# Outward part of a two-layer kernel: eight matmuls, not six, between the first pair of banks and the third pair's products

## The chip, the cores and the metric

One core of a Trainium2 chip runs the kernel. The metric is the device time in microseconds (us) of one execution, as the median of several runs. Differences below 0.2% (about 2.1 us here) can't be told from no change.

## The reference

Three stages run one after the other, all in float32:

```
scores = q @ k^T / sqrt(64) - log(448);  attn = sigmoid(scores);  x = attn @ v      # 4 batches, 12 heads, 448 x 64
x = reshape(x)                                # 1792 tokens x 768 channels
g = relu(x @ w_in)**2;             x = g @ w_out      # layer 0, hidden width 2048
h = x @ w2_in; g = max(h,0) + alpha*min(h,0); out = g @ w2_out   # layer 1, hidden width 2048
```

The document calls the product with w_in of a layer *inward* and the product with w_out *outward*.

## The kernel before, in words

The attention stage takes the first 158 us. The two layers are cut into 32 **units** (`UNITS`, numbered here 0 to 31): layer (2) x half of the tokens, 896 columns (2) x pair of 128-wide blocks of the hidden width (8). Units 0 to 15 are layer 0, units 16 to 31 are layer 1. Each unit has an inward part of 63 matmuls (`product`, L511: seven products k = 0 to 6 of nine matmuls, which give the four quarters of the hidden block pair by additions) and an outward part (`out_product`, L534) of 72 matmuls in layer 0 and 84 in layer 1.

Every operand is held as a high and a low part of type fp32r, so that one float32 product is three matmuls: high by high and high by low of the weights (`HIGH`, two matmuls), and low by high (`LOW`, one matmul). Hidden values are in `G[j]` (j = 0, 1 for the two hidden blocks; halves t = 0, 1 of the tokens), outward weights in `WO[j]`.

The outward results go in **pairs** of output tiles: six pairs per unit in layer 0, seven in layer 1. A pair fills two banks of PSUM, which are one buffer of `two`; there are two such buffers, used in turn. When a pair is complete, one instruction evicts both banks into the accumulator `acc`: L720 on VectorE (DVE) adds to it, L718 on ScalarE (ACT) copies where the unit is the first of its eight (units 0, 8, 16 and 24). So pair 2 (the third) takes the buffer of pair 0, and its first matmul has to wait for pair 0's eviction; pair 3 waits for pair 1's, and so on.

A complete pair needs 12 matmuls: two tiles x two hidden blocks x three. Of the first two pairs, the parts with j = 1 are issued ahead of those with j = 0. From the third pair on, each pair's 12 matmuls follow each other.

A hidden quarter is made on DVE and ACT once its product is out of TensorE (`add_hidden`): in layer 0 an addition (L662, DVE), relu, two squares (L642 to L644, ACT) and the low part `g` (L654, DVE); in layer 1 an addition (L662, DVE), two relus (L650, L651, ACT), a combination with alpha (L652, DVE), a copy to the high part (L653, ACT) and the low part (L654, DVE). The last quarter (from product k = 6: j = 1, t = 0) is made while the outward part has already begun; only pair 3 and later ones read the half t = 0. Weight parts for the next unit are made on the same engines: ACT L236 writes a high part, DVE L240 a low part, DVE L220 to L226 the sums (names `s12`, `s34`, `a1`, `a2`).

The order of instructions on each engine is written out by a planner (`class Plan`) when the program is built. TensorE (PE) keeps the order in which its jobs are added. On the other engines the planner simulates the program with assumed durations (0.2005 us per outward matmul in layer 0 and 0.1735 in layer 1; `dve(cols)` = 0.07 + 0.00105 cols; 0.17 us from the end of a PE job plus 0.10 before a reader may begin) and takes, of the jobs that are ready, the one with the earliest due time. It leaves an engine idle rather than begin a job that would still run when a job with an earlier due time becomes ready:

```
for j in now:
    end = t + jobs[j][1]
    if not any(due[s] < due[j] and begin(s, free[e]) < end and end > due[s] for s in soon):
        return t, j
```

A job counts as `soon` once the last of the jobs that it needs has begun. The due time of an eviction follows from the first matmul that reuses its buffer; that of a weight part from the next unit's products; that of the last quarter's jobs from pair 3. The chip then runs each engine's instructions strictly in the planned order, each when its semaphores allow.

Of the kernel before, what the change touches and what calls it, by code (L numbers as in the profile page):

```python
# [19 lines left out]
class Plan:  # L20
# [11 lines left out]
    def add(self, engine, us, emit, reads=(), writes=(), port=False, size=0):  # L32
        reads, writes = set(reads), set(writes)
        before = {self.last[k] for k in reads | writes if k in self.last}
        for k in writes:
            before |= self.readers.pop(k, set())
        me = len(self.jobs)
        before.discard(me)
        self.jobs.append((engine, us, emit, before, port, size))
        for k in writes:  # L40
            self.last[k] = me
        for k in reads:
            self.readers.setdefault(k, set()).add(me)
# [75 lines left out]
def fused_kernel(ctx: ExitStack, tc: tile.TileContext, q, k, v, w1i, w1o, w2i, w2o, alpha, out):  # L119
# [149 lines left out]
    with tc.manual_schedule():  # L269
# [6 lines left out]
        with tc.tile_pool(name="apool", bufs=1) as apool, tc.tile_pool(name="apsum", bufs=1, space=bass.MemoryType.PSUM) as psum:  # L276
# [145 lines left out]
            for what in X_ORDER[:-1]:  # L422
                i = int(what[1])
# [6 lines left out]
            for d in range(ND):  # L430
                u, w = 2 * d, 2 * d + 1
                i = d - 4
# [69 lines left out]
        HIGH, LOW = ((0, 0), (0, 1)), ((1, 0),)  # L502
# [10 lines left out]
        def outputs(n):  # L513

            if UNITS[n][0] == 0:
                return [[(c, t), (c + 1, t)] for t in (1, 0) for c in range(0, NC, 2)]
            return [[(m, 0), (m, 1)] for m in reversed(range(NM))]

        def sides(n, o):

            if UNITS[n][0] == 0:
                return [o[1]]
            return [t for t in range(2) if o[0] * P < (t + 1) * S and (o[0] + 1) * P > t * S]

        def out_product(n, o, ps, j, ways, begin, end):

            for i, (gi, wi) in enumerate(ways):
                if UNITS[n][0] == 0:
                    c, t = o
                    ops = WO[j][:, wi, c * P:(c + 1) * P], G[j][:, gi, t * S:(t + 1) * S]  # L530
                else:
                    m, e = o
                    ops = G[j][:, gi, m * P:(m + 1) * P], WO[j][:, wi, e * HALF:(e + 1) * HALF]
                nc.tensor.matmul(ps, *ops, start=(begin and i == 0), stop=(end and i == len(ways) - 1), skip_group_check=True)  # L534

        def part_of(n, os):
            layer, p, fp = UNITS[n]
            if layer == 0:
                c, t = os[0]
                cells = [((c + i) * 2 + t) * S // CELL + k for i in range(2) for k in range(S // CELL)]  # L540
                return values_of(p)[:, c:c + 2, t], cells
            m = os[0][0]
            return acc[p][:, m * DM:(m + 1) * DM].rearrange("p (e c) -> p e c", e=2), [m * DM // CELL + k for k in range(DM // CELL)]

        def store(col, rows, channels=slice(0, DM), queues=(nc.sync,)):

            i = at_queue = 0
            while i < P:
                b, at = divmod(col + i, S)
                to = out[b * S:(b + 1) * S, channels]  # L550
                if at < MAIN:
                    r, p = divmod(at, P)
                    n = min(P - i, P - p)
                    to = to[:MAIN].rearrange("(p r) c -> p r c", r=R)[p:p + n, r, :]
                else:
                    n = min(P - i, S - at)
                    to = to[at:at + n, :]
                queues[at_queue % len(queues)].dma_start(out=to, in_=rows[i:i + n])
                at_queue += 1
                i += n  # L560
# [4 lines left out]
        def act(cols):  # L565
            return 0.10 + 0.00083 * cols

        def dve(cols):
            return 0.07 + 0.00105 * cols
# [118 lines left out]
        def add_outward(n):  # L688

            layer, p, fp = UNITS[n]  # L690
            size = HALF if layer else S
            pairs = []
            for os in outputs(n):
                pairs.append((os, at_pair[0] % 2))
                at_pair[0] += 1

            def keys(o, j, ways):
                return [("g", j, t, gi) for gi, _ in ways for t in sides(n, o)] + [key for _, wi in ways for key in ([("wo", j, 0)] if wi == 0 else [("wo", j, 1, e) for e in range(2)])]

            def products(os, b, i, j, ways, begin, end):  # L700
                add("PE", len(ways) * PE_OUT[layer], lambda: out_product(n, os[i], two[b][:, i, :size], j, ways, begin, end), keys(os[i], j, ways), [("o", b)])

            for ways in (HIGH, LOW):
                for os, b in pairs[:2]:
                    for i in range(2):
                        products(os, b, i, 1, ways, ways is HIGH, False)
            for at, (os, b) in enumerate(pairs):
                for i in range(2):
                    if at < 2:
                        products(os, b, i, 0, HIGH + LOW, False, True)  # L710
                    else:
                        products(os, b, i, 0, HIGH + LOW, True, False)
                        products(os, b, i, 1, HIGH + LOW, False, True)
                part, cells = part_of(n, os)
                cells = [("acc", p, cell) for cell in cells]
                both = two[b][:, :, :size]
                if fp == 0:
                    add("ACT", act(2 * size), lambda part=part, both=both: nc.scalar.activation(part, both, AF.Copy), [("o", b)], cells)  # L718
                else:
                    add("DVE", dve(2 * size), lambda part=part, both=both: nc.vector.tensor_add(part, both, part), [("o", b), *cells], cells)  # L720
                if fp == NB - 1 and layer == 1:
                    m = os[0][0]
                    if n < NU - 1:
                        add("SP", 0.1, lambda m=m: store(p * PAIR + m * P, acc[p][:, m * DM:(m + 1) * DM]), cells, [], size=DM * BYTES)
                    else:
                        for e in range(2):
                            add("SP", 0.1, lambda m=m, e=e: store(p * PAIR + m * P, acc[p][:, m * DM + e * HALF:m * DM + (e + 1) * HALF], slice(e * HALF, (e + 1) * HALF), (nc.sync, nc.scalar)), cells, [], size=HALF * BYTES)
# [9 lines left out]
        for n in range(NU):  # L737
# [31 lines left out]
            if n < NU - NB and fp == NB - 1:  # L769
                for i in range(7):  # L770
                    if i < 4:
                        add("SP", 0.05, lambda i=i, to=x_kept[n // NB]: nc.sync.dma_start(out=X[i].bitcast(F32), in_=to[i]), [("x_kept", i, c) for c in range(KH)], [key for c in range(KH) for key in x_keys(i, c)], size=2 * KH * S * BYTES)
                    else:
                        for c in range(KH):
                            add_x_parts(other, i, c, "POOL" if i == 6 else "DVE", (X[i][:, 0, c], X[i][:, 1, c]), x_keys(i, c))
            add_outward(n)
        plan.run()

# [29 lines left out]
```

## Time and profile before

| | us |
|---|---|
| median of 3 runs (lowest, highest) | 1070.81 (1070.32, 1071.83) |
| the profiled execution's own time | 1072.4 |
| its span, first to last instruction | 1070.2 |
| PE busy / DVE busy / ACT busy / POOL busy | 1050.4 / 737.3 / 608.5 / 252.1 |
| mean granted TensorE clock | 0.998 |

A row of a timeline gives the start (us from the span's start), the duration of a group of consecutive like instructions, engine, line, operation, operands, count, and in brackets the idle time of the engine before it with what ended it. Matmuls are pipelined: a single one is shown as some 365 ns (448 columns) or 334 ns (384 columns) long although the next one starts some 200 or 174 ns later. So the idle time in brackets is smaller than the delay of the matmul behind it, which is its start less the start that the even pace would have given.

### The profile page before, as it was taken

To read this page: it belongs to the slowest core of one execution; us is meant where nothing else is said; L and a number is where in the kernel's file an instruction comes from. 1 tells how busy PE (TensorE), PEld (TensorE's weight loads), DVE (VectorE), ACT (ScalarE), POOL (GpSimd) and SP (SyncE) were. 2 spreads that over 40 slices of the span, in tenths; PEclk is the share of its full clock that TensorE was granted. 3 is DMA by queue.
4 is the path that set the end of the run, shared out by engine and by line. 5 is a ranking of instruction groups with operands and counts; after the bars stand their busy time and mean duration, and the time that the engine had idled before them with its cause. 6 is when DMAs were issued, how large, how long until landed. Compare 5 with 4: busy or idle time off the path is not lost. (4 is left out here: it accounts for less than half of the span.)

```text
span 1070.2 us, 14822 instructions
## 1 busy us (share of the span) xinstructions
PE 1050.4 (98%) x5607; PEld 912.3 (85%) x5607; DVE 737.3 (69%) x990; ACT 608.5 (57%) x933; POOL 252.1 (24%) x229
## 2 busy tenths in 40 slices
PE   9999999999999999999999999999999999999998
PEld 5555558888898989888898899999999999999997
DVE  5555976677677775777777686787666756666765
ACT  4567778667666558666565666554443463333432
POOL 0001323253311142542110335431111211111110
PEclk9999999999999999999999999999999999999999
DMA  7577738556655775676655844543115611111103
GB/s 150 147 190 196 199 106 291 156 177 212 228 194 158 260 278 182 201 270 220 202 207 192 324 167 170 184 170 121 48 49 214 207 59 60 60 60 59 51 9 104
DMA packets 126007, 174.78 MB, mean 163 GB/s; under 512 B 55536, under 2 KB 98800, under 8 KB 124272
## 3 DMA queue, kind: packets, MB, share of 16 engines
q1 hardware_dynamic: 123440, 172.59, 49.8%
q10 hardware_dynamic: 2496, 1.25, 0.4%
q8 instruction: 44, 0.72, 0.3%
q14 instruction: 27, 0.22, 0.1%
HBM read 123.87 MB, written 49.94 MB: 162 GB/s over the span
## 5 line engine op out<-in xcount | busy, mean ns | idle before, releaser
L511 PE MATMUL h<-x,wi 128*128 128x448 f32 x2016 | 419.9, 367 | 0.5 <-DVE c L662 0.4
L511 PEld LDWEIGHTS h<-x,wi 128*128 128x128 f32 x2016 | 378.0, 188 | 36.8 <-DVE c L662 1.2
L534 PE MATMUL o<-g,wo 128*128 128x448 f32 x1152 | 244.1, 369 | 10.0 <-DVE acc L720 8.8
L534 PEld LDWEIGHTS o<-g,wo 128*128 128x128 f32 x1152 | 216.2, 189 | 35.3 <-DVE acc L720 14.1
L534 PE MATMUL o<-wo,g 128*128 128x384 f32 x1344 | 240.7, 336 | 2.7 <-DVE acc L720 2.1
L534 PEld LDWEIGHTS o<-wo,g 128*128 128x128 f32 x1344 | 233.0, 188 | 8.8 <-DVE acc L720 6.7
L625 POOL TENSOR_TENSOR wo<-words_o,wo 128x384 fp32r<-128x384 f32 x128 | 128.8, 1038 | 416.6 <-ACT wo L628 369.3
L720 DVE TENSOR_TENSOR acc<-o,acc 128x768 f32<-128x768 f32 (+1 forms) x182 | 182.9, 1015 | 55.1 <-PE o L534 54.2
L662 DVE TENSOR_TENSOR c<-h,c 128x448 f32<-128x448 f32 x160 | 99.6, 623 | 164.6 <-PE h L511 160.6
L628 ACT ACTIVATE wo<-words_o 128x768 fp32r<-128x768 f32 x64 | 50.8, 838 | 188.0 <-issue 128.5
L654 DVE TENSOR_TENSOR g<-c,g 128x448 fp32r<-128x448 f32 x128 | 82.8, 656 | 25.6 <-ACT c L644 22.8
L352 ACT ACTIVATE a<-sc,bias 128x896 f32<-128x896 f32 x72 | 69.2, 1004 | 35.6 <-PE av L370 22.6
L264 POOL TENSOR_TENSOR stage<-acc,stage 128x448 fp32r<-128x448 f32 x36 | 45.3, 1258 | 183.2 <-ACT stage L261 183.2
L236 ACT ACTIVATE wi<-sums 128x768 fp32r<-128x768 f32 x64 | 53.3, 837 | 48.1 <-PE h L511 30.5
L190 ACT ACTIVATE raw<-raw 128x768 f32<-128x768 f32 x64 | 57.8, 904 | 16.0 <-DMA raw<-in_moe_w_in_dram 11.5
L240 DVE TENSOR_TENSOR wi<-sums,wi 128x768 fp32r<-128x768 f32 x64 | 61.0, 956 | 5.9 <-ACT wi L236 5.6
L370 PE MATMUL av<-a,v 128*64 128x448 f32 x288 | 59.4, 548 | 0.0
L192 ACT ACTIVATE raw<-raw 128x768 int32<-128x768 uint32 x64 | 57.6, 900 | 0.0
L650 ACT ACTIVATE pos<-c 128x448 f32<-128x448 f32 x48 | 27.8, 578 | 51.1 <-DVE c L662 50.2
L257 POOL TENSOR_TENSOR acc<-acc 128x448 f32<-128x448 f32 x40 | 53.6, 1348 | 11.4 <-DMA acc<-late 9.5
L240 DVE TENSOR_TENSOR wi<-words_i,wi 128x768 fp32r<-128x768 f32 x64 | 50.1, 786 | 6.6 <-ACT wi L236 4.7
L652 DVE SCALAR_TENSOR_TENSOR c<-c,nal,pos 128x448 f32<-128x448 f32 x64 | 43.4, 678 | 8.2 <-ACT c L651 8.0
(75 smaller groups left out, 847.0 us busy)
## 6 DMA issues: line engine op xcount, KB each, us to landing
raw<-in_moe_w_in_dram SPq DMA_DIRECT2D x32, 768.0 KB, 5.7
raw<-in_moe_w_out_dram SPq DMA_DIRECT2D x32, 768.0 KB, 5.2
kept_x<-stage SPq DMA_DIRECT2D x36, 448.0 KB, 3.5
x<-kept_x SPq DMA_DIRECT2D x12, 1344.0 KB, 11.2
v<-in_v_dram SPq DMA_DIRECT2D x24, 192.0 KB, 2.9
nat<-in_q_dram SPq DMA_DIRECT2D x22, 192.0 KB, 3.4
nat<-in_k_dram SPq DMA_DIRECT2D x20, 192.0 KB, 3.3
late<-held SPq DMA_DIRECT2D x12, 224.0 KB, 2.2
```

The lines of the kernel that those rows point to most:

```text
L190: nc.scalar.activation(half.bitcast(F32), half.bitcast(F32), AF.Prelu, scale=2.0 ** -112, alpha=2.0 ** 32)
L192: nc.scalar.activation(half, half.bitcast(U32), AF.Copy, scale=2.0 ** -29 * (1 - 2.0 ** -12), bias=-0.5 + 7.5 * 2.0 ** -12)
L240: nc.vector.tensor_sub(lo, w, hi)
L257: eng.tensor_sub(to, x, y)
L352: nc.scalar.activation(sig[u, j], ps[:, :, :S], AF.Sigmoid, bias=bias[:, :1], scale=SCALE)
L370: nc.tensor.matmul(avs[u][h * D:(h + 1) * D, :S], vals[u][:, h, j, :], a[:, h, :], start=(u % 2 == 0 and j == 0), stop=(u % 2 == 1 and j = ...
L511: nc.tensor.matmul(ps, W[:, wp, at:at + P], X[k][:, xp, c], start=(k < 3 and c == 0 and i == 0), stop=(c == KH - 1 and i == 2), skip_group ...
L534: nc.tensor.matmul(ps, *ops, start=(begin and i == 0), stop=(end and i == len(ways) - 1), skip_group_check=True)
L625: nc.gpsimd.tensor_sub(WO[j][:, 1, at], words["o"][:, j, at], WO[j][:, 0, at])
L654: add("DVE", dve(S), lambda: nc.vector.tensor_sub(gl, e, gh), [key, h_key], [l_key], port=True)
L662: add("DVE", dve(S), lambda: nc.vector.tensor_add(to, bank(b), other), [("h", b), other_key], [key])
L720: add("DVE", dve(2 * size), lambda part=part, both=both: nc.vector.tensor_add(part, both, part), [("o", b), *cells], cells)
```

## The change

The order of the first 24 outward matmuls of every unit is changed, and nothing else. Before: HIGH parts with j = 1 of pairs 0 and 1 (8 matmuls), their LOW parts (4), pair 0's six matmuls with j = 0, pair 1's six. After: HIGH parts with j = 1 of pairs 0 and 1 (8), then pair 0's LOW parts (2) and its six with j = 0, then pair 1's LOW parts (2) and its six. So pair 0 is complete after 16 matmuls, not 18, and pair 1 after 24 as before. All other engines' jobs are the same, and the planner orders them anew.

```diff
-            for ways in (HIGH, LOW):
-                for os, b in pairs[:2]:
+            for os, b in pairs[:2]:
+                for i in range(2):
+                    products(os, b, i, 1, HIGH, True, False)
+            for at, (os, b) in enumerate(pairs):
+                if at < 2:
                     for i in range(2):
-                        products(os, b, i, 1, ways, ways is HIGH, False)
-            for at, (os, b) in enumerate(pairs):
+                        products(os, b, i, 1, LOW, False, False)
                 for i in range(2):
                     if at < 2:
                         products(os, b, i, 0, HIGH + LOW, False, True)
```

## Rows read from the trace of the kernel before

**Rows 1.** Waits of PE: line, releaser, us in total, times, longest.
```profile
PE o L534 <- DVE acc L720: 11.0, 25, 2.4
```
**Rows 2.** Chain that ended last, around unit 26: start, us, engine, tile, line.
```profile
913.72 0.56 DVE wi L240
914.27 0.88 DVE acc L720
```
**Rows 3.** Timeline of PE, units 9 and 26, the next inward part last.
```profile
430.20 5.02 PE L534 MATMUL o<-g,wo 128*128 128x448 f32 x24
435.74 10.00 PE L534 MATMUL o<-g,wo 128*128 128x448 f32 x48 [0.52 <-DVE acc L720]
445.58 12.93 PE L511 MATMUL h<-x,wi 128*128 128x448 f32 x63
...
910.69 4.33 PE L534 MATMUL o<-wo,g 128*128 128x384 f32 x24
915.20 10.69 PE L534 MATMUL o<-wo,g 128*128 128x384 f32 x60 [0.18 <-DVE acc L720]
925.73 13.18 PE L511 MATMUL h<-x,wi 128*128 128x448 f32 x63
```
**Rows 4.** Timeline of DVE, units 9 and 26.
```profile
434.06 0.62 DVE L654 TENSOR_TENSOR g<-c,g 128x448 fp32r<-128x448 f32 x1 [0.59 <-ACT c L644]
434.60 2.08 DVE L720 TENSOR_TENSOR acc<-o,acc 128x896 f32<-128x896 f32 x2
...
912.96 0.68 DVE L652 SCALAR_TENSOR_TENSOR c<-c,nal,pos 128x448 f32<-128x448 f32 x1
913.72 0.56 DVE L240 TENSOR_TENSOR wi<-words_i,wi 128x384 fp32r<-128x384 f32 x1
914.19 1.82 DVE L720 TENSOR_TENSOR acc<-o,acc 128x768 f32<-128x768 f32 x2
915.93 1.15 DVE L654 TENSOR_TENSOR g<-c,g 128x448 fp32r<-128x448 f32 x2
```
**Rows 5.** Timeline of DVE, unit 31: its first two evictions.
```profile
1054.23 2.00 DVE L720 TENSOR_TENSOR acc<-o,acc 128x768 f32<-128x768 f32 x2 [0.49 <-PE o L534]
```
**Rows 6.** Timeline of DVE, unit 1, and of DVE, unit 14.
```profile
204.04 0.62 DVE L654 TENSOR_TENSOR g<-c,g 128x448 fp32r<-128x448 f32 x1 [0.73 <-ACT c L644]
...
576.20 0.56 DVE L240 TENSOR_TENSOR wi<-words_i,wi 128x384 fp32r<-128x384 f32 x1 [0.53 <-ACT wi L236]
```
**Rows 7.** Timeline of ACT, unit 0, ahead of and with its first eviction.
```profile
175.94 0.83 ACT L236 ACTIVATE wi<-sums 128x768 fp32r<-128x768 f32 x1
176.68 0.89 ACT L718 ACTIVATE acc<-o 128x896 f32<-128x896 f32 x1
```
**Rows 8.** Timeline of PE, units 2 and 3, and the inward part behind.
```profile
237.08 7.53 PE L534 MATMUL o<-g,wo 128*128 128x448 f32 x36 [0.53 <-DVE acc L720]
...
257.21 5.02 PE L534 MATMUL o<-g,wo 128*128 128x448 f32 x24
264.61 11.70 PE L534 MATMUL o<-g,wo 128*128 128x448 f32 x48 [2.38 <-DVE acc L720]
276.15 13.18 PE L511 MATMUL h<-x,wi 128*128 128x448 f32 x63
```
**Rows 9.** Timeline of DVE, unit 3.
```profile
261.24 0.96 DVE L240 TENSOR_TENSOR wi<-words_i,wi 128x768 fp32r<-128x768 f32 x1
262.93 0.62 DVE L654 TENSOR_TENSOR g<-c,g 128x448 fp32r<-128x448 f32 x1 [0.73 <-ACT c L644]
```
**Rows 10.** Windows, unit 3: stretch, length, busy (PE, PEld, DVE, ACT, POOL), clock, DMA.
```profile
264.61:267.30 2.69, 2.69 (x8) 2.41 (x9) 2.27 (x3) 2.69 (x5) 0.00 (x0) 0.58 0.03 6
```
**Rows 11.** Timelines of unit 17: DVE, POOL, PE.
```profile
662.90 2.80 DVE L654 TENSOR_TENSOR g<-c,g 128x448 fp32r<-128x448 f32 x2
...
663.80 2.91 POOL L257 TENSOR_TENSOR acc<-acc 128x448 f32<-128x448 f32 x2
...
665.76 7.75 PE L534 MATMUL o<-wo,g 128*128 128x384 f32 x43 [0.45 <-DVE g L654]
```

## The prediction

> **What bounds the kernel now.** I read the busy times first: PE is busy for 1050.4 of 1070.2 us, DVE for 737.3 and ACT for 608.5, so only what delays PE can move the end. Then the waits of PE: nearly all of them are outward matmuls that wait for an eviction on DVE, 25 waits and 11.0 us [rows 1]. The chain of waits says the same for one unit: a weight part on DVE, then the eviction, then 60 matmuls [rows 2].
>
> The waits understate it, since a matmul is drawn longer than the distance to the next. The timeline of PE gives the true delay. In unit 26 (layer 1) the first 24 matmuls last 4.33 us; less one matmul's 0.334 and divided by 23 that is a pace of 0.1737. The 25th should start at 910.69 + 24 x 0.1737 = 914.86 and starts at 915.20: 0.34 late. The 60 from there to the inward part take 925.73 - 915.20 = 10.53, 0.11 more than 60 x 0.1737. So the unit loses 0.45 [rows 3]. In unit 9 (layer 0) the pace is (5.02 - 0.365) / 23 = 0.2024, the 25th is 435.74 - 435.06 = 0.68 late, and the same 0.11 follows: 0.79 [rows 3]. This sum over the 32 units gives 20.3 us, of which unit 3 has 2.6.
>
> **Why the eviction is late: the order on DVE.** In unit 26 pair 0's last matmul is drawn until 913.98 (start 910.69, 17 paces, one matmul of 0.334), yet the first of the two evictions, each some 0.96 long, begins at 914.19, behind a weight part of 0.56 that began at 913.72 [rows 4]. In unit 9 pair 0 is through by 434.01, and the eviction begins at 434.60 behind the low part of the last quarter, which had come at 434.06 after 0.59 of idling [rows 4]. Only where DVE has nothing else, as in unit 31, does it begin at once: 1054.23, when pair 0 is through at 1054.20 [rows 5].
>
> **The change, step by step.**
>
> *Matmuls.* None is added or removed, each has its own weight load before and after: 0. Operands: the parts with j = 0 are wanted two matmuls (0.35 to 0.41) sooner, pair 1's LOW parts later. In unit 26 all that these read was made before the outward part began or in its first 0.4 us, against 10 matmuls = 1.74 us: 0. Only unit 0, whose last such low part comes closest, may lose up to 0.2.
>
> *Two matmuls more of cover.* Pair 0 is complete 2 x 0.1737 = 0.35 (layer 1) or 0.40 (layer 0) sooner. If the eviction then begins at once, it is over in unit 26 at 910.69 + 2.94 + 0.03 + 0.96 = 914.62, ahead of the 25th matmul's 914.86 and about when its weight load would go. In unit 9: 430.20 + 3.41 + 0.03 + 1.09 = 434.73, against 435.06. So stall and the 0.11 behind it (a weight load that isn't hidden) both vanish: not 0.35 but all of 0.45 or 0.79.
>
> *Does it begin at once?* That hangs on the planner, by its own assumed times (used for the order only). Layer 0: the eviction used to become ready 18 x 0.2005 + 0.27 = 3.88 after the first outward matmul, now 3.48. The low part of the last quarter takes 0.54 in its reckoning; in the planner's listing of the kernel before it begins between 2.98 and 3.32 in units 3 to 7 and 9 to 13, so it would end after 3.48. An eviction with an earlier due time then holds it back (the quoted loop), and DVE takes the eviction first. In units 1, 14 and 15 the low part begins at 2.61 to 2.81 and stays ahead. In units 14 and 15 another job (from 3.76) stood between it and the eviction; this one now goes behind. Layer 1: ready at 16 x 0.1735 + 0.27 = 3.05, not 3.39; the combination L652 of the last quarter (2.53 to 3.14 in the listing) and the weight part (3.27) both go behind it.
>
> *The sum for layer 0*, from each unit's delay as above: units 4 to 7 and 9 to 13 lose nothing any more, nine units of 0.36 to 0.79, together 5.8. Units 14 and 15 (weight part or x part ahead of the eviction [rows 6]) 2.2. Unit 1: the low part runs at 204.04, after pair 0 would be through, and the eviction stays behind it [rows 6]: 0. Units 0 and 8, where ACT evicts: the weight copy of 0.83 ahead [rows 7] goes behind; ACT is free only at about 175.9, so 0.75 and 0.5. Unit 2: DVE is free 0.46 sooner, and the second eviction, now behind a weight part (0.76 of delay before the 37th matmul [rows 8]), goes ahead of it: 1.2. Unit 3: the 25th matmul is 264.61 - 262.07 = 2.5 late, since the low part comes at 262.93 only [rows 8, 9]. With the eviction behind the weight part of 261.24, which lasts until 262.2, about 1.3 remains. The ten matmuls after the stall run at a granted clock of 0.58 [rows 10], near the lower of the two levels (1.2 of 2.4 GHz), and cost 1.6; nothing like it follows delays of up to 1 us elsewhere. I take that clock loss as gone: 2.8 (bounds 1.3 and 3.0). Layer 0: 13.2.
>
> *The sum for layer 1.* Eleven units with a job between (18, 20 to 23, 25 to 30), nine of 0.45, one 0.53, one 0.56: 5.1. Units 16, 24 and 31: 0.8. Units 17 and 19: 0, next paragraph. Layer 1: 5.9.
>
> *What is late next.* The last quarter's chain goes behind the eviction. In unit 26 L652 moves from 912.96 to about 914.5 and the two low parts end about 917.2, against 917.08 before [rows 4]. Pair 3's LOW part, the 42nd matmul, is due at 910.69 + 41 x 0.1737 = 917.81, its weight load at 917.6: 0.4 of slack. In unit 17 it is gone already: the two low parts take 2.80 instead of 1.15, while POOL works (663.80), and the 42nd matmul waits for them [rows 11]. There the gain is given back, in units 17 and 19. The Trainium skill (SBUF — State Buffer, Who interferes with whom) has a rule that makes more of this: a DVE instruction with two SBUF inputs contends with a GpSimd instruction that reads SBUF, one with at most one SBUF input does not. By it the evictions, which read PSUM, never stretch, while L652 and L654, which the change moves later, stretch wherever POOL is at work, units 17 to 19; with unit 18 given back too the sum would be 0.5 less.
>
> *Pace.* Matmuls of 448 columns run in one of two paces that last until a stall: (12.93 - 0.365) / 62 = 0.2027 in one inward part [rows 3], (13.18 - 0.368) / 62 = 0.2066 in another [rows 8]. Which comes after a stall I can't foretell. Without stalls from unit 4 on one pace would hold for 12 x 135 = 1620 matmuls, of which some 900 now have the faster: all slow costs 3.5, all fast gives 2.8. I take 0.
>
> *Total.* 13.2 + 5.9 = 19.1, less 1.6 for small new waits that another order brings (bounds 0 and 4): 17.5. The profiled execution took 1072.4, 1.6 above the median of 1070.8; 1072.4 - 17.5 = 1054.9 there, 1053.3 for the median. I say 1053.5.
>
> **The rivals.**
>
> 1. *The order on the engines stays.* The eviction is ready sooner but still stands behind the low part or the weight part. For it: 0.35 to 0.4 is little, and the parts that stand ahead begin 0.03 and 0.26 us before or around pair 0's end [rows 4]. Against it: the planner's rule, and its margins (3.48 falls inside the span of the low part in ten units; only unit 13's margin is as small as 0.04). Only units 16, 17, 19, 24 and 31 would gain, 1.4 in all: 1069.4. The Trainium skill (TensorE: Matmul & The Clock Gate, Architectural detail) says that ACT and DVE are strict first-in first-out: by that, the case hangs on the written order alone.
>
> 2. *Stalls move from the 25th to the 42nd matmul in layer 1.* If L652 goes behind both evictions (1 us later still), the low parts end about 918.0 and the 42nd matmul is 0.3 late: of 5.9 only 1 or 2 remain, and layer 0 with its pace slow gives 9.5: about 1060.
>
> 3. *Slower.* As in 2, but with ACT taking two weight copies (0.83 each) before the copy L653, since the quarter comes so late. The low part would end 1.7 us later, about 919.7, the 42nd matmul 2.0 late instead of the 0.45 now: 16 x 1.55 = 25 lost against 13 gained, 1083. It decides from the point at which the low part ends more than 1.7 us after 917.08, and the whole kernel is slower from 1.3 of new delay per unit. Against it: L653's due time is by far the earlier.
>
> 4. *Pace* all slow or all fast: 1057 or 1050.5, within the forecast's own range.
>
> **How the numbers follow.** Forecast (order flips in most units, 1048 to 1059): 0.72. Rival 1: 0.11. Rival 2: 0.09. Rival 3: 0.05. Below 1048 (all of the 20 and the fast pace): 0.03. The range for 8 in 10 takes in the forecast and most of rival 2: 1048 to 1064. Faster by over 0.2% (about what a measurement can tell from no change): forecast, rival 2, below, and a little of rival 1: 0.86. Same: 0.09. Slower: 0.05.
>
> **What would show it.** Right: in unit 26's place the first eviction starts 0.03 after the 16th matmul's end with the last quarter's L652 and the weight part behind it; PE's waits for L720 fall from 11.0 to under 3; unit 1 keeps its stall; unit 3's clock stays full. Wrong: evictions that still begin behind L654 or L240, or a new row of waits of PE for L654.

## The result, and the profile after

The changed kernel takes 1059.14 us as the median of 4 runs (1058.57 to 1059.38), the kernel before 1071.15 beside it: ratio 0.9887, 95% interval 0.987 to 0.9905, so 12.0 us less. The forecast was 1053.5 with a range of 1048 to 1064: right in direction and inside the range, but 5.6 us too hopeful. The profiled execution took 1058.57, its span 1056.8, 13.4 less than before.

The waits of PE in the changed kernel (the eviction on DVE is now line 722, that on ACT line 720):

```profile
PE o L534 <- DVE acc L722: 3.4, 6, 1.1
PE h L511 <- DVE c L662: 2.7, 4, 1.0
PE o L534 <- ACT acc L720: 1.8, 2, 1.3
```

Against [rows 1], the waits for DVE evictions fell from 11.0 to 3.4 (the prediction had named under 3 as the sign of being right). New is the second row: inward matmuls that wait for DVE additions, 0.4 us before.

Layer 1 went nearly as foreseen. Timelines of PE and of DVE in unit 26, to be held against [rows 3, 4]:

```profile
899.21 14.85 PE L534 MATMUL o<-wo,g 128*128 128x384 f32 x84
913.90 1.40 PE L511 MATMUL h<-x,wi 128*128 128x448 f32 x6
```
```profile
901.82 0.63 DVE L654 TENSOR_TENSOR g<-c,g 128x448 fp32r<-128x448 f32 x1 [0.26 <-ACT g L653]
902.36 0.95 DVE L722 TENSOR_TENSOR acc<-o,acc 128x768 f32<-128x768 f32 x1
903.23 0.68 DVE L652 SCALAR_TENSOR_TENSOR c<-c,nal,pos 128x448 f32<-128x448 f32 x1
903.82 0.95 DVE L722 TENSOR_TENSOR acc<-o,acc 128x768 f32<-128x768 f32 x1
```

The 84 matmuls need 913.90 - 899.21 = 14.69 us, 15.04 before; at the even pace it would be 14.59. The weight part is gone from in front of the eviction, and L652 has gone behind it. But another job stands there now: the low part of the quarter from k = 5 (L654), so the eviction starts at 902.36 and not at 902.18. It ends in time for the 25th matmul (903.38), not for its weight load, which idles 0.15 us and begins at 903.37, just after the eviction's end at 903.31; the 26th matmul is 0.10 late. This 0.10 is left in ten units, 0.18 to 0.24 in units 17 to 19, nothing in 16, 24 and 31.

Layer 0 split in two. In units 2, 3, 4, 6 and 10 the eviction went ahead of the last quarter's low part and the delay is gone, but for 0.16 in unit 3. Unit 10, PE and then DVE of unit 2:

```profile
454.10 14.76 PE L534 MATMUL o<-g,wo 128*128 128x448 f32 x72
468.69 1.58 PE L511 MATMUL h<-x,wi 128*128 128x448 f32 x7
```
```profile
232.51 1.09 DVE L722 TENSOR_TENSOR acc<-o,acc 128x896 f32<-128x896 f32 x1 [0.50 <-PE o L534]
233.52 0.61 DVE L654 TENSOR_TENSOR g<-c,g 128x448 fp32r<-128x448 f32 x1
234.12 1.09 DVE L722 TENSOR_TENSOR acc<-o,acc 128x896 f32<-128x896 f32 x1
```

468.69 - 454.10 is 72 times 0.2026: nothing lost, and in unit 2 DVE waited for PE, not PE for DVE. In units 5, 7, 9 and 12 to 15 (and in unit 1, as forecast) the last quarter's low part kept its place. In unit 11 it went behind, but a weight part for which DVE idled 1.15 us stands there instead, and the delay grew from 0.78 to 1.00. In units 0 and 8, where ACT evicts, 0.73 and 1.58 are left. Unit 12, PE, DVE and ACT:

```profile
509.81 15.11 PE L534 MATMUL o<-g,wo 128*128 128x448 f32 x72
524.76 5.44 PE L511 MATMUL h<-x,wi 128*128 128x448 f32 x26
```
```profile
511.56 0.96 DVE L240 TENSOR_TENSOR wi<-words_i,wi 128x768 fp32r<-128x768 f32 x1
513.25 0.62 DVE L654 TENSOR_TENSOR g<-c,g 128x448 fp32r<-128x448 f32 x1 [0.73 <-ACT c L644]
513.79 1.08 DVE L722 TENSOR_TENSOR acc<-o,acc 128x896 f32<-128x896 f32 x1
```
```profile
511.43 0.56 ACT L642 ACTIVATE c<-c 128x448 f32<-128x448 f32 x1
512.02 0.58 ACT L643 ACTIVATE g<-c 128x448 fp32r<-128x448 f32 x1
512.64 0.58 ACT L644 ACTIVATE c<-c 128x448 f32<-128x448 f32 x1
```

Pair 0 was through at 513.22. DVE idled 0.73 us for ACT, then made the low part, then evicted, 0.57 late. The unit takes 524.76 - 509.81 = 14.95, 0.36 more than unit 10.

To see where the time went I took the starts of all matmuls of the units and compared each distance with 0.2027 (448 columns) or 0.1735 (384): what the 25th and 26th matmul of an outward part are late; other gaps over 0.045 us; and the rest, which is the slower pace. In us, good to about 0.1, from the profiled execution of each:

| kernel | median | 25th, layer 0 | 25th, layer 1 | other gaps | slower pace |
|---|---|---|---|---|---|
| before | 1071.15 | 13.7 | 6.6 | 4.6 | 7.2 |
| changed | 1059.14 | 8.5 | 1.6 | 4.3 | 4.2 |
| x1_order | 1061.95 | 9.1 | 4.3 | 2.8 | 6.1 |
| x2_cover | 1070.19 | 13.7 | 5.8 | 5.0 | 6.4 |
| x3_act | 1047.47 | 0.3 | 0.3 | 3.7 | 3.4 |
| x4_twelve | 1050.76 | 0.3 | 0.0 | 5.8 | 4.6 |
| x5_act_six | 1059.05 | 4.9 | 4.7 | 3.6 | 6.5 |
| x6_nopool | 1049.98 | 2.0 | 1.8 | 1.0 | 4.1 |
| x8_act_twelve | 1052.36 | 0.0 | 0.0 | 6.4 | 4.8 |
| x9_act_nopool | 1051.85 | 0.0 | 0.6 | 2.2 | 5.2 |
| x10_memset | 1053.13 | 5.0 | 1.5 | 0.5 | 5.7 |

From before to changed: 5.2 + 5.0 + 0.3 + 3.0 = 13.5, the 13.4 of the span.

The medians were taken on several chips, on which the kernel before took 1070.11 to 1071.41. The ratios given below are each to the kernel before on the same chip, so two experiments are best compared by their ratios (0.001 is 1.1 us).

### The profile page after: what moved, and what is told of

Read it like the earlier page. It is cut to its first block, busy times and chain, and to the rows that moved or that the text cites. A ratio compares the mean times of both kernels' runs of the same rounds, so it can differ in the third digit from the quotient of the medians.

```text
span 1056.8 us, 14833 instructions
## 1 busy us (share of the span) xinstructions
PE 1041.5 (99%) x5607; PEld 911.7 (86%) x5607; DVE 744.0 (70%) x990; ACT 606.8 (57%) x933; POOL 254.0 (24%) x229
## 4 chain that ended last, share of the span: by engine, by line
PE 82%; ACT 9%; DVE 4%; DMA 2%; issue 2%; SPq 0%; POOL 0%; ACTq 0%; DVEq 0%
PE o L534 39%; PE h L511 30%; PE av L370 5%; PE sc L350 4%; ACT g L643 2%; ACT c L644 2%; ACT c L642 2%; ACT wi L236 1%; PE tp L317 1%; PE av L378 1%; DVE acc L722 1%; PE scr L360 1%; DVE c L662 1%; PE tp L320 1%; DMA raw<-in_moe_w_in_dram 1%
## 5 line engine op out<-in xcount | busy, mean ns | idle before, releaser
L511 PE MATMUL h<-x,wi 128*128 128x448 f32 x2016 | 419.1, 367 | 2.7 <-DVE c L662 2.7
L511 PEld LDWEIGHTS h<-x,wi 128*128 128x128 f32 x2016 | 378.0, 188 | 38.3 <-DVE c L662 4.8
L534 PE MATMUL o<-g,wo 128*128 128x448 f32 x1152 | 239.4, 367 | 5.4 <-DVE acc L722 3.4
L534 PE MATMUL o<-wo,g 128*128 128x384 f32 x1344 | 237.6, 336 | 0.0
L625 POOL TENSOR_TENSOR wo<-words_o,wo 128x384 fp32r<-128x384 f32 x128 | 130.2, 1049 | 394.4 <-ACT wo L628 391.4
L662 DVE TENSOR_TENSOR c<-h,c 128x448 f32<-128x448 f32 x160 | 99.4, 622 | 139.5 <-PE h L511 130.7
L654 DVE TENSOR_TENSOR g<-c,g 128x448 fp32r<-128x448 f32 x128 | 80.9, 632 | 33.7 <-ACT c L644 27.4
L264 POOL TENSOR_TENSOR stage<-acc,stage 128x448 fp32r<-128x448 f32 x36 | 46.4, 1288 | 188.4 <-ACT stage L261 164.2
L240 DVE TENSOR_TENSOR wi<-sums,wi 128x768 fp32r<-128x768 f32 x64 | 63.7, 997 | 8.0 <-ACT wi L236 7.6
L257 POOL TENSOR_TENSOR acc<-acc 128x448 f32<-128x448 f32 x40 | 54.8, 1372 | 10.8 <-DMA acc<-late 8.7
L240 DVE TENSOR_TENSOR wi<-words_i,wi 128x768 fp32r<-128x768 f32 x64 | 52.0, 814 | 6.4 <-ACT wi L236 4.8
L652 DVE SCALAR_TENSOR_TENSOR c<-c,nal,pos 128x448 f32<-128x448 f32 x64 | 43.4, 678 | 7.7 <-ACT c L651 7.5
```

What stands on the lines that cost most here:

```text
L240: nc.vector.tensor_sub(lo, w, hi)
L511: nc.tensor.matmul(ps, W[:, wp, at:at + P], X[k][:, xp, c], start=(k < 3 and c == 0 and i == 0), stop=(c == KH - 1 and i == 2), skip_group ...
L625: nc.gpsimd.tensor_sub(WO[j][:, 1, at], words["o"][:, j, at], WO[j][:, 0, at])
L654: add("DVE", dve(S), lambda: nc.vector.tensor_sub(gl, e, gh), [key, h_key], [l_key], port=True)
L662: add("DVE", dve(S), lambda: nc.vector.tensor_add(to, bank(b), other), [("h", b), other_key], [key])
```

## The experiments

**Order or cover?** Two kernels take the change apart. In x1_order the planner sees the changed order, but PE issues pair 1's LOW matmuls where they stood before; in x2_cover it is the other way round.

Against the changed kernel, in x1_order pair 1's LOW jobs issue nothing, and pair 0's first job with j = 0 issues them:

```diff
+                    if how == "first":
+                        for other in early.pop("low"):
+                            other()
+                    if how != "done":
                         out_product(n, os[i], two[b][:, i, :size], j, ways, begin, end)
```

Against the kernel before, in x2_cover pair 1's first job with j = 0 issues them:

```diff
+                    if how == "first":
+                        for c in range(2):
+                            out_product(n, os[c], two[b][:, c, :size], 1, LOW, False, False)
```

> DVE, ACT and POOL run in the order that the planner wrote for the changed kernel, PE in the order of the kernel before (pair 0 complete after 18 matmuls, six of cover). Theory (the new order on DVE carries most of the gain): every first eviction starts no sooner than pair 0's end, 0.35 to 0.40 us later than in the changed kernel where it started at once there; layer 0 keeps its delays and adds about 0.2 in five units, layer 1 has about 0.28 a unit instead of 0.10: some 4 us above the changed kernel, 1063, 8 below the kernel before. Rival (the two matmuls of cover carry it): about the kernel before, 1069 to 1071.

> PE in the order of the changed kernel (pair 0 complete after 16 matmuls), DVE, ACT and POOL in the order that the planner wrote for the kernel before. Theory (order): evictions stay behind the low part in layer 0 and the weight part in layer 1, so the 25th matmul is late as before; only units 16, 17, 19, 24 and 31 gain, 1.4 us together: about 1069.5. Rival (cover): 0.35 to 0.40 in each of 32 units, 11 to 12 us: about 1059.

x1_order: 1061.95, ratio 0.992 (0.9908 to 0.9932), 8 us below the kernel before. x2_cover: 1070.19, ratio 0.9997 (0.9988 to 1.0006), no gain. The order of the other engines alone brings two thirds of the change, the two matmuls alone nothing, and the remaining 4 us come only where both are there. DVE in unit 9 of x2_cover shows why (the eviction is line 727 here):

```profile
432.95 0.95 DVE L240 TENSOR_TENSOR wi<-sums,wi 128x768 fp32r<-128x768 f32 x1
434.50 0.63 DVE L654 TENSOR_TENSOR g<-c,g 128x448 fp32r<-128x448 f32 x1 [0.60 <-ACT c L644]
435.04 2.08 DVE L727 TENSOR_TENSOR acc<-o,acc 128x896 f32<-128x896 f32 x2
```

The sequence is that of [rows 4], idle time and all: a pair that is ready sooner changes nothing for an instruction that stands behind another. In units 17, 19 and 31, where nothing stood ahead, the delays of 0.28 to 0.35 did go to nothing; units 16 and 24, which the expectation also named, gained nothing.

**Why seven units of layer 0 kept the old order.** In the traces a relu and the two squares behind it start some 0.60 us apart on ACT (511.43, 512.02 and 512.64 in unit 12 above); the planner reckons 0.47.

```diff
-                ready[s] = max(ready[s], t + us if jobs[s][0] == e and e != "SP" else end + self.HOP)
+                ready[s] = max(ready[s], t + us + (0.13 if e == "ACT" else 0.0) if jobs[s][0] == e and e != "SP" else end + self.HOP)
```

> The changed kernel; only the planner is told that an ACT job which needs the ACT job before it begins 0.13 us later, as the traces show (relu to square to square start 0.60 apart where the planner assumes 0.47). Theory (ten units of layer 0 keep their delay since the planner believes the last quarter's low part is done before the eviction is ready, and on the chip it comes 0.9 us later): with the longer chain the low part ends after 3.48 in the planner's time, the eviction goes ahead of it in most of those units, and PE's waits for L722 fall from 3.4 to under 1.5: 4 to 6 us less than the changed kernel, about 1054. Rival (the delays there have another cause, such as weight parts or DMA): within 1 us of the changed kernel.

1047.47, ratio 0.979 (0.9774 to 0.9806): 11.7 below the changed kernel by the medians, 10.4 by the ratios, twice the expectation. Layer 0 alone gained 8.2 at the 25th matmul, units 0, 8 and 11 with it, layer 1 gained 1.3 and the pace 0.8. The 25th matmul is late in two units only, 0.6 us in all. Unit 12, DVE:

```profile
503.23 0.62 DVE L654 TENSOR_TENSOR g<-c,g 128x448 fp32r<-128x448 f32 x1
504.93 1.09 DVE L722 TENSOR_TENSOR acc<-o,acc 128x896 f32<-128x896 f32 x1 [1.09 <-PE o L534]
505.94 0.61 DVE L654 TENSOR_TENSOR g<-c,g 128x448 fp32r<-128x448 f32 x1
506.56 1.09 DVE L722 TENSOR_TENSOR acc<-o,acc 128x896 f32<-128x896 f32 x1
```

DVE now waits for pair 0, evicts, and only then makes the last low part. The same correction with six matmuls of cover:

> The kernel before with its order of matmuls (six of cover); only the planner is told of the 0.13 us between dependent ACT jobs. Theory (what decides is which side of the low part the planner puts the eviction): the low part then ends after 3.88 in the planner's time in most units of layer 0, evictions go ahead of it, and the 25th matmul is 0.2 to 0.3 late instead of 0.8; unit 3's clock loss goes too: stall sum 8 to 10 instead of 20.3, about 1057. Rival (the correction helps only where the cover is eight): the order stays, 1068 to 1071.

1059.05, ratio 0.9884 (0.9864 to 0.9905): as much as the change itself, without its order of matmuls. Most units lose 0.2 to 0.35, the eviction's own length beyond six matmuls (unit 2 loses 1.5). So with the planner corrected, the two more matmuls, with the order that the planner then writes for them, are worth 11.6 us by the medians and 10.1 by the ratios; with the order of before they were worth nothing.

**More cover.** Pairs 0 and 1 one after the other.

```diff
-            for os, b in pairs[:2]:
-                for i in range(2):
-                    products(os, b, i, 1, HIGH, True, False)
             for at, (os, b) in enumerate(pairs):
                 if at < 2:
+                    for i in range(2):
+                        products(os, b, i, 1, HIGH, True, False)
```

> Pairs 0 and 1 one after the other, so that pair 0 is complete after 12 matmuls and 12 stand between. Theory: the eviction is ready 0.8 us (layer 0) or 0.7 (layer 1) sooner than in the changed kernel, ahead of the last quarter's low part in every unit; the delay of the 25th matmul is gone nearly everywhere (10.1 us in the changed kernel), but pair 0 now wants the low part of j = 0, t = 1 at the 9th matmul, 1.6 us after the first, which in units 0 and 3 comes later than that: 7 to 9 us below the changed kernel, about 1051. Rival (new waits for hidden values at the 7th to 9th matmul, and evictions that push the hidden chain back): no gain or a loss, 1058 to 1064.

> Corrected planner and twelve matmuls of cover together. Theory (x3_act has already lost all but 0.6 us of the delay of the 25th matmul, so cover is worth nothing more): within 2 us of x3_act, 1046 to 1050. Rival (cover and order are separate gains that add): 1040 or less.

x4_twelve: 1050.76, ratio 0.9826 (0.9806 to 0.9847), as expected: with twelve the delay is gone though the planner is wrong. With both corrections, x8_act_twelve: 1052.36, ratio 0.9833 (0.9795 to 0.9871), no better than x3_act and 2.4 outside what was expected. Its delay at the 25th matmul is zero, but its other gaps are 6.4, of which 2.3 are waits for low parts (L654). Cover and order are two ways to the same gain.

**The new waits of inward matmuls.** In unit 10's inward part PE waits a microsecond for L662. PE, DVE and POOL there:

```profile
448.52 5.74 PE L511 MATMUL h<-x,wi 128*128 128x448 f32 x27 [1.01 <-DVE c L662]
```
```profile
444.51 1.52 DVE L222 TENSOR_TENSOR sums<-sums,words_i 128x384 f32<-128x384 f32 x1
445.95 1.51 DVE L224 TENSOR_TENSOR sums<-words_i 128x384 f32<-128x384 f32 x1
447.39 0.54 DVE L226 TENSOR_TENSOR sums<-words_i,sums 128x384 f32<-128x384 f32 x1
447.86 0.61 DVE L662 TENSOR_TENSOR c<-h,c 128x448 f32<-128x448 f32 x1
```
```profile
444.47 1.15 POOL L264 TENSOR_TENSOR stage<-acc,stage 128x448 fp32r<-128x448 f32 x1
445.69 1.36 POOL L257 TENSOR_TENSOR acc<-acc 128x448 f32<-128x448 f32 x1
```

Three like sums take 1.52, 1.51 and 0.54 us; the two long ones lie beside POOL instructions. That the rule of the Trainium skill which the prediction names (SBUF — State Buffer, Who interferes with whom) would strike here, in the inward part, I had not seen. The trace agrees with it: 1.5 us beside POOL instructions that read, 0.54 without. x10_memset keeps every order and lets POOL only write where it made the x sums and the kept x parts (the low parts of outward weights, L625, it still computes):

```diff
-            add(engine, ..., lambda: x_sum(p, i, c, nc.gpsimd if engine == "POOL" else nc.vector), ...)
+            add(engine, ..., lambda: nc.gpsimd.memset(x_block(p, X_SUM[i][0], c), 0.0), ...)
...
-            add(engine, ..., lambda: x_low(p, i, c, hi, lo, ...), ...)
+            add(engine, ..., lambda: nc.gpsimd.memset(lo.bitcast(F32), 0.0) if engine == "POOL" and i < 4 else x_low(p, i, c, hi, lo, ...), ...)
```

> The changed kernel with the same order of instructions on every engine; only the x sums (L257) and the low parts of x into stage (L264) on POOL are replaced by fills with zero, which read nothing. It leaves out that part of the second half's input. Theory (DVE sums with two operands in SBUF stretch from 0.55 to 1.5 us while a POOL instruction reads SBUF, and this is what delays L662 and makes inward matmuls wait in units 2, 3, 10 and 18): the sums L220 to L226 stay under 0.7 except beside L625, PE's waits of L511 for L662 fall from 2.7 to under 0.5, and the kernel is 3 to 4 us faster than the changed one, about 1055.5; the delay of the 25th matmul stays at 10. Rival (the order written for DVE is late by itself): the waits stay, 1058 to 1060.

1053.13, ratio 0.9835 (0.982 to 0.9849): 6 us below the changed kernel, more than expected. The same sums in unit 10's inward part:

```profile
441.07 0.55 DVE L222 TENSOR_TENSOR sums<-sums,words_i 128x384 f32<-128x384 f32 x1
441.54 0.55 DVE L224 TENSOR_TENSOR sums<-words_i 128x384 f32<-128x384 f32 x1
442.01 0.55 DVE L226 TENSOR_TENSOR sums<-words_i,sums 128x384 f32<-128x384 f32 x1
```
```profile
441.06 0.48 POOL L588 MEMSET stage<- 128x448 f32 x1
441.47 0.48 POOL L583 MEMSET acc<- 128x448 f32 x1
```

The fills lie beside the first two sums, and none of the sums that lie beside fills alone takes over 0.56 us. No wait of L511 for L662 is left, and the other gaps fall from 4.3 to 0.5. The part that missed: I had expected the 25th matmul to stay 10 us late in all; it fell to 6.5. Units 8 and 9 lost 1.6 and 1.3 in the changed kernel and lose 0.0 and 0.1 here: there ACT was late after stretched DVE instructions (two sums of 1.40 in unit 8; in unit 9 a weight part, L240, of 1.91 instead of 0.95), and the eviction behind it. Another run keeps the result whole and moves that work to DVE:

```diff
-            add_x_parts(p, i, c, "POOL", (stage[:, 0], stage[:, 1]), keys)
+            add_x_parts(p, i, c, "DVE", (stage[:, 0], stage[:, 1]), keys)
...
-                            add_x_sum(other, int(what[1]), c, "POOL")
+                            add_x_sum(other, int(what[1]), c, "DVE")
```

> The changed kernel with the x sums (L257) and the kept x parts (L264 into stage) computed on DVE instead of POOL. Theory (the new waits of inward matmuls for L662, 2.7 us, come from DVE sums that take 1.5 instead of 0.55 us while POOL works): without POOL work no DVE sum is over 0.7 us, the waits of L511 for L662 in units 2, 10 and 18 (1.2, 1.3 and 0.8 with what follows) vanish; DVE gets some 72 jobs of 0.62 more, which it has room for: 2 to 4 us less, about 1056. Rival (DVE is simply behind in those units, POOL or not): the waits stay or grow with the extra work, 1058 to 1063.

1049.98, ratio 0.9797 (0.9781 to 0.9814). The waits for L662 are gone, but most of the 9 us is another thing: the planner wrote a new order in which more evictions go first (25th matmul 3.8 us late in all). So this run does not price the contention; x10_memset does, though its fills are also shorter than what they replace. Both corrections together:

> Corrected planner and no x work on POOL in the units (it goes to DVE). Theory (x3_act still has 3.7 us of other delays, 1.8 of them in unit 18 where DVE and POOL work at once): these vanish, 2 to 3 us less than x3_act, about 1045. Rival (the extra DVE work pushes evictions and hidden values back again): 1047 to 1051.

1051.85 (1048.42 to 1053.3), ratio 0.9827 (0.9811 to 0.9843): not below x3_act, though its gaps are smaller (2.8 against 4.3 us); its pace is slower by 1.7. The spread of its runs is wide, and I leave it open.

**The pace.** In x3_act inward parts of layer 1 run at the slower pace in 15 of 16 units. x7_nudge puts one small matmul ahead of each:

```diff
+            if k == 0 and n >= 16:
+                nc.tensor.matmul(spare[:, :32 * (n % 8 + 1)], W[:, 0, :P], X[0][:, 0, 0, :32 * (n % 8 + 1)], start=True, stop=True, skip_group_check=True)
```

> The kernel with the corrected planner (x3_act), and in layer 1 one extra small matmul into a spare bank ahead of each inward part, 32 x (unit mod 8 + 1) columns wide, so 32 to 256. It adds 16 matmuls to what is computed, whose results nobody reads. Theory (the pace of 448-column matmuls, 0.2027 or 0.2066, is set by how the stretch begins): in some widths the 63 inward matmuls run at 0.2027 and take 12.8 instead of 13.0 us, and units with the same width agree. Rival (the pace after 384-column matmuls is always the slow one): all sixteen inward parts at 0.2066, and the kernel 1 to 3 us slower than x3_act.

1048.47 from 2 runs (1047.38 and 1049.56), no difference that can be told from x3_act. But the pace is another. PE in unit 25 and the inward part behind, x3_act and then x7_nudge:

```profile
861.34 14.77 PE L534 MATMUL o<-wo,g 128*128 128x384 f32 x84
875.95 13.18 PE L511 MATMUL h<-x,wi 128*128 128x448 f32 x63
888.96 14.73 PE L534 MATMUL o<-wo,g 128*128 128x384 f32 x84
```
```profile
861.46 14.75 PE L537 MATMUL o<-wo,g 128*128 128x384 f32 x84
876.05 0.21 PE L509 MATMUL spare<-x,wi 128*128 128x96 f32 x1
876.10 12.98 PE L514 MATMUL h<-x,wi 128*128 128x448 f32 x63
888.92 14.75 PE L537 MATMUL o<-wo,g 128*128 128x384 f32 x84
```

The 63 matmuls take 12.82 us, not 13.01, and even with the extra matmul the unit is 0.16 shorter (27.46 against 27.62). Fifteen of sixteen inward parts ran fast, at all eight widths; the sixteenth, unit 19, began fast and turned slow at the 37th matmul. So what stands at the start of a stretch can set its pace. Why is not shown, and only one execution of this kernel was profiled.

## Why the prediction was right, and by how much it was off

**The order decides whether the 0.35 to 0.40 us of cover count**: shown by x1_order and x2_cover. The cover alone gave nothing, the order alone 8 of the 12 us, and 4 need both. Rival 1 priced the order that stays at 1069.4; x2_cover, which is that case, measured 1070.19.

**"Layer 0: 13.2" was mis-sized.** The 25th matmul gained 5.2 of the 10.8 that the sum had for it. The failing step is "in the planner's listing of the kernel before it begins between 2.98 and 3.32": I let the low part keep its place in the planner's time while the rest moved. In the new plan it is done at 3.2 to 3.46, just before 3.48, in units 5, 7, 9, 12 and 13 (in 7, 9, 12 and 13 ACT makes one weight copy fewer ahead of the last quarter), and the eviction stays behind it. So only five of the ten units for which I had forecast the flip made it: 3, 4, 6, 10 and 11. On the chip the low part ends at 4.06 to 5.02 (unit 12: 513.87 - 509.81 = 4.06). In units 14 and 15 I had let the low part stay ahead and still counted the whole delay as gone: 0.64 and 0.36 are left. An eviction behind L654 or L240 was the sign that I had given for being wrong, and units 5, 7, 9 and 11 to 15 show it. x3_act, which corrects that one assumed time, removes the delay.

By units, the shortfall of 5.6 is about 3.0 in units 5, 7, 11, 12 and 13, 1.0 in units 14 and 15, 0.4 in unit 0 and 2.9 in units 8 and 9, which lost 1.6 and 1.3 instead of nothing; units 2 and 3 did 1.6 better than the sum. The loss of units 8 and 9 belongs to the DVE instructions stretched beside POOL: in x10_memset, with the same order, it is gone (in x3_act too, by another order). Unit 1 kept 0.74, as said. Unit 3 kept 0.16 where I had said 1.3, its clock stayed at 1.00, and unit 2's second delay is gone.

**"Layer 1: 5.9" was about right**: 5.0 at the 25th matmul. The step "begins at once" was off by 0.2 us, since L654 stands ahead, which costs 0.10 in ten units. L652 went behind the first eviction as said, and the 42nd matmul never waited, in unit 17 neither: the gain that I had given back there came, 0.9 us in unit 17.

**"Small new waits: 1.6"** were 3.8 of gaps in the inward parts of units 2, 3, 10 and 18, against 0.7 (unit 11) before: larger than taken, inside the bounds of 0 and 4, and in a place that I had not looked at. The gaps that went with the old kernel (units 2, 3, 7, 11 and 17) make up for them; those of units 2 and 3 the sum for layer 0 had counted.

**"Pace: I take 0"** was 3.0 of gain, near the 2.8 given for all fast: in the changed kernel every inward part of units 0 to 15 ran fast. That was luck, since I had said that I can't foretell the pace; without it the miss would have been over 8 us. The premise that a pace lasts until a stall did not hold everywhere: in x3_act's unit 19 the inward part went from 0.2066 to 0.2027 after some 36 matmuls, with no stall there.

Rivals 2 and 3 (hidden values too late in layer 1) did not come, in any unit.

## What to carry to other kernels

An instruction that is ready sooner gains nothing if it stands in a fixed order behind one that waits: before counting on more cover, read what runs just ahead of the late instruction, and what that one waited for. Where a planner writes the order, its assumed durations are part of the kernel; one figure that was 0.13 us too small for dependent ACT instructions cost nearly as much here as the whole change brought (10.4 us by the ratios against 12.0). And when one order is rewritten, all are: a forecast that moves one job and keeps the others in place is too hopeful.

## What the runs showed of the hardware that I had not expected

- DVE sums of 384 columns with both operands in SBUF took up to 1.55 us instead of 0.55 beside POOL instructions that read SBUF, and 0.55 in the same place of the order beside POOL fills, which only write. Not every one was stretched: in the changed kernel two sums that lie wholly beside one L264 took 0.56, and that L264 took 2.12 instead of some 1.2.
- Matmuls of 448 columns run at 0.2027 or 0.2066 us apart at a granted clock of 1.00, mostly for whole stretches; with one small matmul ahead of each stretch 15 of 16 ran at the faster instead of one.
- An idle time of 2.38 us on PE was followed by a granted clock of 0.58 [rows 8, 10], one of 1.83 us (unit 3 of x2_cover) by a clock of 0.50 (from 266.2 to 268.0), the lower level; after one of 1.31 us (unit 8 of the changed kernel) and one of 1.90 us (unit 18 of x4_twelve) the clock stayed at 1.00. So the length of the idle time alone does not tell whether the clock falls.
